# Regrouping the last batch's dense pieces, an earlier gather and a late register read in a fused sparse-attention and expert kernel

## Chip, cores and metric

The kernel runs on one NeuronCore of a Trainium2 chip. The metric is the device time of one execution in microseconds. The median of three runs of the kernel before is 246.15 us (246.1 to 246.69).

## What is computed

A chunk-sparse causal attention, then a layer of eight experts with a dense residual branch. Cut to what matters:

```python
# attention: q, k, v are (4, 8, 768, 64); chunks of 32 keys, the 6 best chunks per query
ub = sum(maximum(q * k_min, q * k_max))           # bound of a chunk's scores
top_chunks = argsort(where(causal, ub, -1e9))[..., -6:]
attn = softmax(where(in_top_chunk & (i >= j), q @ k.T / 8, -1e9))
x = (attn @ v) as rows (3072 tokens, 512)

# experts: 8 experts, 512 -> 512 -> 512, each token goes to one
y_dense = relu(x @ w1_dense) @ w2_dense
e = argmax(x @ w_gate, axis=1); gate_w = softmax(x @ w_gate)[e]
y_moe[mask_e] = gate_w * (relu(x[mask_e] @ w1[e]) @ w2[e])
out = y_dense + y_moe                              # (3072, 512) float32
```

## The kernel before

**Attention.** The four batches run one after the other, each as four pairs of heads. Between the attention steps of a batch the expert layer's work on the batch before is interleaved: transposes of x, the gate, the ranks of the tokens within their experts, and the dense branch. For every token its row of x, its gate weight and its token number are scattered into a table in DRAM, sorted by expert. What is left after the last attention step is the last batch's share of this work and all expert blocks.

**Expert blocks.** The table is read in blocks of 128 rows, each of one expert. `N1 = 11` blocks are full before the last batch is known; up to `N2 = 20` more follow. `NOFT = 28` blocks are always done; three rare ones stand in a conditional at the end, `tc.If(total > N2 - RARE)`, where `total` is a count that the program computes (`nblk`) and that every engine reads into a register. For block i the steps are:

- `fetch(i)` (line 498): SyncE loads the block's rows from the table into `xg`; the last block, 27, has a tile `xl` of its own and is fetched ahead of 11 (`order`).
- `own(i)` (line 513): VectorE copies the expert's first weights to a fixed place (`w`).
- `tx(i)` (line 856): TensorE transposes the rows, VectorE copies them out (858).
- `e1(i)` (865): sixteen matmuls of the first layer; ScalarE applies relu (868).
- `e2(i)` (886): four matmuls of the second layer; ScalarE multiplies by the gate weight (893); GpSimd scatters the 128 result rows and adds them to the output in DRAM (895).

TensorE's program order in loop step i is e1(i), tx(i+1), the step's extra work, e2(i-1).

**The extra work.** The last batch's dense branch is 28 pieces: two groups of 384 tokens, each eight half pieces of the first layer (408, two matmuls each) and six half pieces of the second layer (424, two matmuls each). Every second piece of the second layer ends in a ScalarE copy to a tile `ys` (429) and two SyncE writes to the output (433). The pieces are dealt to loop steps from 1 on by the line with `extra.setdefault`. In steps 0 to 2 also stand the last batch's transposes, gate, ranks, its six table scatters (388) on GpSimd, and SyncE's eight writes of empty rows to the table (914).

**Orders that are written out.** Fetches of blocks from 11 on begin in step 8, and each is ordered behind the latest dense write emitted so far (`latest["ys"]`). SyncE works its queue in order. GpSimd's scatters are in block order.

**The last block's dense rows.** The scatter of block 27 doesn't add: `dense_rows(27)` (878) gathers the dense results of its 128 tokens from the output beforehand into `dr`, on GpSimd's queue behind the latest scatter, and VectorE adds them (891) before the scatter, which overwrites. The gather must find all dense writes of the batch done. It stands in step 12.

**The count.** In step 9 all five engines read `nblk` (line 954; a TENSOR_LOAD in each engine's own queue). A similar read (line 470) fetches the packed list of experts, on TensorE and VectorE, in step 8 for the blocks from 11 on.

Of the kernel before, what the change touches and what calls it, by code (L numbers as in the profile page):

```python
# [7 lines left out]

# [9 lines left out]
def kernel(  # L18
# [12 lines left out]
    nc = tc.nc  # L31
# [25 lines left out]
    N1 = (N * (B - 1) // B - E * 127 + 127) // 128  # L57
    N2 = NBLK - N1
# [107 lines left out]
    nblk = const.tile([1, 1], mybir.dt.int32)  # L166
# [80 lines left out]
    def apart(dma, group, reason):  # L247

        if group in groups:
            tc.declare_no_dep(dma.ins, group=group, reason=reason)  # L250
        groups.add(group)
        tc.add_to_no_dep_group(group, dma.ins)
# [227 lines left out]
    def load_offs():  # L480

        for have, engine in ((offs, mybir.EngineType.PE), (offs1, mybir.EngineType.DVE)):
            have.extend(unpack((eo, eparts[engine]), EF, 3, NK * 512, engine, (E - 1) * NK * 512,
                               "the expert of a block is at most the last"))
# [7 lines left out]
    def fetch(i):  # L492
        if i == NBLK - RARE - 1:
            xg = eg.tile([128, XW], U16, name="xl", bufs=1)
        else:
            xg = eg.tile([128, XW], U16, name="xg")
        es[i]["x"] = xg
        ld = nc.sync.dma_start(out=xg, in_=table[bass.ds(rows[i], 128)])
        if i < N1:
            tc.add_to_no_dep_group("full", ld.ins)  # L500
# [5 lines left out]
    def own(i):  # L506
        if i < 1:
            w = eg.tile([128, NK, 512], HF, name="w1a", bufs=1)
        else:
            w = later[0].tile([128, NK, 512], HF, name="w1", bufs=2)  # L510
        es[i]["w1"] = w
        with tc.issue_after(latest["xT"].ins) if "xT" in latest else nullcontext():
            nc.vector.tensor_copy(w.rearrange("p j f -> p (j f)"), w1f[:, bass.ds(offs1[i], NK * 512)])  # L513

    FIRST = 6
    with (
# [131 lines left out]
        h = None  # L648
        for d16, src in ((k16, s0["k"]), (q16, s0["q"])):
            o = d16.rearrange("p t g d -> p g t d")  # L650
            nc.gpsimd.tensor_copy(o[:, :, 0:3], src[:, :, 0:3])
            with after(h) if h else ExitStack():
                h = nc.scalar.copy(o[:, :, 3:6], src[:, :, 3:6])
            if src is s0["k"]:
                with after(h):
                    h = nc.scalar.copy(kT[0][0][64:128], exf)
# [27 lines left out]
        def place_k(p, g, pk):  # L684
            return nc.scalar.copy(kT[p][g][64 * g : 64 * g + 64].rearrange("d (T p j) -> d T p j", p=128, j=NJ),
                                  pk[64 * g : 64 * g + 64].rearrange("d (T j p) -> d T p j", p=128, j=NJ))
# [9 lines left out]
        with after(h):  # L696
            h = nc.scalar.activation(qp, pq, AF.Relu)
# [4 lines left out]
        for g in range(2):  # L702
            with after(h):
                h = place_k(0, g, pk)
        with after(dv):
            prep_ub(0)
        with after(h):
            h = nc.scalar.copy(kT[0][1][0:64], exf)
# [26 lines left out]
        with after(scored[-1][1]):  # L735
            h = nc.scalar.activation(qp, pq, AF.Relu)
# [102 lines left out]
    with (  # L839
# [8 lines left out]
        a, d, ranks, places, _ = batch_fills(B - 1)  # L848
# [3 lines left out]
        def tx(i):  # L852
            s = es[i]
            tp = p1.tile([128, NK, 128], HF, name="tp", tag="tr")
            for ko in range(NK):
                nc.tensor.transpose(tp[:, ko], s["x"][:, ko * 128 : (ko + 1) * 128].bitcast(HF), ident)  # L856
            s["xT"] = xT = et.tile([128, NK, 128], HF, name="exT")
            latest["xT"] = nc.vector.tensor_copy(xT, tp)  # L858

        def e1(i):  # L860
            s = es[i]
            hp = p2.tile([128, NK, 128], FP, name="hp", tag="h")
            for j in range(NK):
                for ko in range(NK):
                    nc.tensor.matmul(hp[:, j], s["w1"][:, ko, j * 128 : (j + 1) * 128], s["xT"][:, ko],  # L865
                                     start=(ko == 0), stop=(ko == NK - 1), skip_group_check=True)
            s["hT"] = h = et.tile([128, NK, 128], HF, name="ehT")
            nc.scalar.activation(h, hp, AF.Relu)  # L868

        def tokens(i):  # L870
            return bass.IndirectOffsetOnAxis(ap=es[i]["x"][:, Dm + 2 : Dm + 4].bitcast(mybir.dt.int32), axis=0)

        def dense_rows(i):

            es[i]["dense"] = dr = et.tile([128, Dm], FP, name="dr", bufs=1)
            nc.gpsimd.memset(dr, 0.0)
            with tc.issue_after(latest["pool"].ins):
                ga = nc.gpsimd.indirect_dma_start(out=dr, out_offset=None, in_=out, in_offset=tokens(i),
                                                  bounds_check=N - 1, oob_is_err=False)
            apart(ga, "add", "every token is in one block")  # L880

        def e2(i):
            s = es[i]
            yp = p3.tile([128, Dm], FP, name="yp", tag="y")
            for j in range(NK):
                nc.tensor.matmul(yp, s["hT"][:, j], w2f[:, bass.ds(offs[i] + j * 512, 512)],  # L886
                                 start=(j == 0), stop=(j == NK - 1))
            o = et.tile([128, Dm], FP, name="yo", bufs=5)
            gate, to = s["x"][:, Dm : Dm + 2].bitcast(FP), tokens(i)
            if "dense" in s:  # L890
                nc.vector.scalar_tensor_tensor(o, yp, gate, s["dense"], ALU.mult, ALU.add)
            else:
                nc.scalar.mul(o, yp, gate)  # L893
            with tc.issue_after(latest["put"].ins) if i == 0 else nullcontext():
                sc = nc.gpsimd.indirect_dma_start(out=out, out_offset=to, in_=o, in_offset=None, bounds_check=N - 1,  # L895
                                                  oob_is_err=False,
                                                  compute_op=ALU.bypass if "dense" in s else ALU.add)
            latest["pool"] = sc
            apart(sc, "add", "every token is in one block")
            if i < N1:  # L900
                tc.declare_no_dep(sc.ins, group="dense", reason="the first blocks hold no token of the last batch")
                tc.add_to_no_dep_group("add1", sc.ins)

        def empty():
# [7 lines left out]
            for e in range(E):  # L912
# [2 lines left out]
                apart(z, "rows", "these rows are no token's")  # L915
                tc.declare_no_dep(z.ins, group="full", reason="the first blocks end before these rows")

        AHEAD = 8
        READY = 8
        for i in range(1, 1):  # L920
# [2 lines left out]
        extra = {0: a[:NT] + [a[NT], ranks], 1: list(places)}  # L923
        extra[2] = [empty]
        for n, f in enumerate(d):
            extra.setdefault(1 + n * (N1 - 2) // len(d), []).append(f)
        got = FIRST

        NOFT = NBLK - RARE
# [1 line left out]
        for i in range(NOFT):  # L931
            while got < min(i + AHEAD + 2 + (i >= READY), NOFT, N1 + 3 * max(i - READY + 1, 0)):
                if got < N1:
                    fetch(order[got])
                else:
                    with tc.issue_after(latest["ys"].ins):
                        fetch(order[got])
                got += 1
            if 1 <= i + 1 < NOFT:
                own(i + 1)  # L940
            e1(i)
            if i + 1 < NOFT:
                tx(i + 1)
            for f in extra.get(i, ()):
                f()
            if i > 0:
                e2(i - 1)
            if len(offs) < min(i + 4, NBLK):
                load_offs()
            if i == N1 + 1:  # L950
                dense_rows(NOFT - 1)
            if i == READY + 1:
                with tc.issue_after(latest["rows"].ins):
                    total = nc.values_load_multi_w_load_instructions(
                        nblk, min_val=0, max_val=N2, bass_reorder=False,
                        skip_runtime_bounds_check_because="the blocks that are left are at most N2")[1][0]
        e2(NOFT - 1)
        with tc.If(total > N2 - RARE):
            for i in range(NOFT, NBLK):
                fetch(i)  # L960
                latest.pop("xT", None)
                own(i)
                tx(i)
                e1(i)
                e2(i)
# [30 lines left out]
```

## Time and profile before

| | |
|---|---|
| median of 3 runs | 246.15 us |
| profiled execution, its own time | 247.56 us |
| its span, first to last instruction | 245.9 us |
| mean granted TensorE clock | 0.983 |
| TensorE busy | 211.6 us (86%) |
| VectorE busy | 175.4 us (71%) |
| ScalarE busy | 174.3 us (71%) |
| GpSimd busy | 162.9 us (66%) |
| DMA | 50.55 MB, mean 206 GB/s |

The chain of waits follows the work that ended last back to the start, each step to what released it; "issue" in it is time in which an engine waited for nothing that the profile shows. In a timeline, the bracket behind a row is the idle time of that engine before it and what ended it. POOL is GpSimd, PE TensorE, DVE VectorE, ACT ScalarE, SP SyncE; a q behind the name means the engine's instruction queue. L886 is line 886 of the kernel before.

### The profile page before, as it was taken

Reading aid. Unit: us, or ns where it says so; the run is one execution under the profiler, and the core shown is the slowest. Engines: PE = TensorE matmul, PEld = TensorE weight load, DVE = VectorE, ACT = ScalarE, POOL = GpSimd, SP = SyncE. Lnnn points to the kernel's source line nnn. Section 1 sums busy time; section 2 is a strip of 40 time slices with the busy share of each in tenths; the row PEclk is TensorE's granted clock in tenths of the full one; section 3 lists DMA queues with packets and bytes.
Section 4 is the critical chain, followed back from the end, with each engine's and each line's share of the span. In section 5 each row is a group of like instructions: output and inputs, shape, how many; then the busy total and the mean of one; then the engine's idle time right before and its main releaser. Section 6 shows DMA issues by size and latency. Waiting matters only on the chain.

```text
span 245.9 us, 7890 instructions
## 1 busy us (share of the span) xinstructions
PE 211.6 (86%) x2771; PEld 149.6 (61%) x2771; DVE 175.4 (71%) x561; ACT 174.3 (71%) x325; POOL 162.9 (66%) x213
## 2 busy tenths in 40 slices
PE   1688878898997999988999996989999989999950
PEld 0466556676666676755667764667666557777720
DVE  3889999999989789797798996577723335555510
ACT  4579797897887898696899786644556556666630
POOL 6457997785379687268877517330688757888881
PEclk9999999999999999999999998899999999999996
DMA  6999999999899999979999946147589999968785
GB/s 174 247 268 279 210 240 251 270 214 265 222 168 358 182 300 261 263 128 251 296 177 256 188 82 182 42 119 197 157 267 215 222 250 254 204 130 122 88 122 106
DMA packets 68279, 50.55 MB, mean 206 GB/s; under 512 B 29712, under 2 KB 61328, under 8 KB 68240
## 3 DMA queue, kind: packets, MB, share of 16 engines
q1 hardware_dynamic: 53008, 30.72, 47.0%
q0 software_dynamic: 15232, 19.32, 45.8%
q8 instruction: 23, 0.38, 0.6%
q14 instruction: 16, 0.13, 0.2%
HBM read 41.93 MB, written 18.23 MB: 245 GB/s over the span
## 4 chain that ended last, share of the span: by engine, by line
PE 35%; POOL 16%; DVE 14%; issue 12%; ACT 10%; DMA 10%; POOLq 1%; SPq 0%; DVEq 0%; ACTq 0%
ACT ex L608 6%; PE yp L886 6%; PE hp L865 6%; PE hp L408 5%; POOL ex L610 4%; DMA out_dram<-yo,xg 4%; DVE ks L546 4%; PE sp L604 4%; POOL table L388 4%; PE yp L424 4%; DMA xg<-table 2%; PE op L623 2%; DMA qf<-in_q_dram 2%; ACT kp L543 2%; PE tp L856 2%
## 5 line engine op out<-in xcount | busy, mean ns | idle before, releaser
L608 ACT ACTIVATE ex<-sp 128x512 f16<-128x512 f32 (+1 forms) x176 | 91.5, 613 | 10.3 <-PE sp L604 8.5
L604 PE MATMUL sp<-rT,kT 128*128 128x128 f16 (+3 forms) x384 | 64.3, 262 | 4.3 <-ACT ex L608 1.1
L610 POOL TENSOR_SCALAR_AFFINE_SELECT ex<-ex 128x512 f16<-128x512 f16 x48 | 32.4, 685 | 37.7 <-ACT ex L608 25.6
L895 POOL DMA_INDIRECT out_dram<-yo,xg x27 | 44.8, 1660 | 12.0 <-issue 5.2
L623 PE MATMUL op<-v,ex 128*128 128x65 f16 x672 | 45.9, 194 | 7.2 <-POOL ex L610 5.6
L623 PEld LDWEIGHTS <-ex 128*128 128x128 f16 x672 | 35.9, 98 | 23.1 <-POOL ex L610 10.0
L388 POOL DMA_INDIRECT table<-xbig,slot x24 | 24.3, 1012 | 18.5 <-issue 18.5
L858 DVE COPY exT<-tp 128x512 f16<-128x512 f16 x28 | 11.8, 423 | 32.8 <-PE tp L856 31.5
L604 PEld LDWEIGHTS <-kT 128*128 128x128 f16 x384 | 28.5, 98 | 8.4 <-issue 5.2
L886 PE MATMUL yp<-we,ehT 128*128 x112 | 30.9, 379 | 0.4 <-ACT ys L429 0.2
L865 PEld LDWEIGHTS <-w 128*128 128x128 f16 x432 | 26.4, 98 | 7.9 <-issue 2.2
L408 PE MATMUL hp<-xT,wd 128*128 128x384 f16 x128 | 30.2, 341 | 0.6 <-DVE xT L264 0.6
L865 PE MATMUL hp<-exT,w 128*128 128x128 f16 x432 | 29.2, 219 | 0.7 <-issue 0.7
L893 ACT ACTIVATE yo<-yp,xg 128x512 f32<-128x512 f32 x27 | 18.5, 687 | 14.0 <-PE yp L886 13.2
L546 DVE TENSOR_REDUCE ks<-kp 128x24 f16<-128x768 f16 x28 | 25.5, 945 | 3.7 <-ACT kp L543 3.5
L424 PE MATMUL yp<-wd,hT 128*128 128x512 f16 x96 | 25.7, 379 | 0.3
L868 ACT ACTIVATE ehT<-hp 128x512 f16<-128x512 f32 x28 | 16.7, 597 | 12.1 <-PE hp L865 9.0
L413 ACT ACTIVATE hT<-hp 128x384 f16<-128x384 f32 x30 | 15.0, 498 | 12.0 <-PE hp L408 11.4
L513 DVE COPY w<-we 128x2048 f16 x27 | 18.7, 693 | 0.2 <-DVE exT L858 0.2
L634 DVE TENSOR_TENSOR xbig<-op,rs 128x384 f16<-128x384 f32 x32 | 17.5, 547 | 0.3
L429 ACT COPY ys<-yp 128x512 f32<-128x512 f32 x21 | 12.8, 609 | 6.3 <-PE yp L424 6.0
L886 PEld LDWEIGHTS <-ehT 128*128 128x128 f16 x112 | 10.2, 97 | 10.3 <-issue 3.6
(158 smaller groups left out, 371.6 us busy)
## 6 DMA issues: line engine op xcount, KB each, us to landing
we<-in_moe_w_dram POOLq DMA_DIRECT2D x16, 512.0 KB, 6.6
kf<-in_k_dram SPq DMA_DIRECT2D x32, 192.0 KB
qf<-in_q_dram SPq DMA_DIRECT2D x32, 192.0 KB
vf<-in_v_dram SPq DMA_DIRECT2D x32, 192.0 KB
out_dram<-ys SPq DMA_DIRECT2D x48, 128.0 KB
xg<-table SPq DMA_DIRECT2D x27, 136.0 KB
table<-zt SPq DMA_DIRECT2D x9, 136.0 KB
wd<-in_moe_w_dense_dram POOLq DMA_DIRECT2D x2, 512.0 KB, 6.3
```

What stands on the lines that cost most here:

```text
L388: sc = nc.gpsimd.indirect_dma_start(out=table, out_offset=bass.IndirectOffsetOnAxis(ap=keep["slot"][:, t : t + 1], axis=0), in_=xbig[b % 2 ...
L408: nc.tensor.matmul(hp, wd[:, ko, j * 128 : (j + 1) * 128], xT[:, ko, g * G * 128 : (g + 1) * G * 128], start=(ko == 0), stop=(ko == NK - 1))
L424: nc.tensor.matmul(yp, hold["h"][:, j, i * 128 : (i + 1) * 128], wd[:, NK + j], start=(j == 0), stop=(j == NK - 1))
L513: nc.vector.tensor_copy(w.rearrange("p j f -> p (j f)"), w1f[:, bass.ds(offs1[i], NK * 512)])
L546: nc.vector.tensor_reduce(out=ks[:, i], in_=kp.rearrange("d (c w) -> d c w", w=32), op=op, axis=mybir.AxisListType.X)
L604: last = nc.tensor.matmul(sp[:, o : o + w], kT[p % NB][g][:, kt * 128 : (kt + 1) * 128], rT[p % NB][g][:, a * 128 : z * 128], start=(o == ...
L608: scored.append((last, nc.scalar.activation(ex[:, 0:o], sp[:, 0:o], AF.Exp, scale=-0.125)))
L610: latest["pool"] = nc.gpsimd.affine_select(out=ex, in_=ex, compare_op=ALU.is_ge, fill=0.0, base=0, pattern=[[0, 4], [1, 2], [2, 64]], chan ...
L623: nc.tensor.matmul(s["op", g][:, t * (D + 1) : (t + 1) * (D + 1)], ex[:, o : o + 128], v16[p % NB][:, g, kt, :], start=first, stop=(last_o ...
L865: nc.tensor.matmul(hp[:, j], s["w1"][:, ko, j * 128 : (j + 1) * 128], s["xT"][:, ko], start=(ko == 0), stop=(ko == NK - 1), skip_group_che ...
L886: nc.tensor.matmul(yp, s["hT"][:, j], w2f[:, bass.ds(offs[i] + j * 512, 512)], start=(j == 0), stop=(j == NK - 1))
L895: sc = nc.gpsimd.indirect_dma_start(out=out, out_offset=to, in_=o, in_offset=None, bounds_check=N - 1, oob_is_err=False, compute_op=ALU.by ...
```

## The change

Three edits. The 28 dense pieces of the last batch are dealt to seven loop steps (1 to 7) instead of nine (1 to 9), four to each. The gather of the last block's dense rows moves from step 12, behind the scatter of block 11, to step 10, behind the scatter of block 9, the tenth. TensorE's read of the block count moves from step 9 to behind the last e2; the other engines keep theirs in step 9, and the registers of both reads are put together into one value for the conditional.

```diff
+        def count(engines):
+            return nc.values_load_multi_w_load_instructions(
+                nblk, engines=engines, min_val=0, max_val=N2, bass_reorder=False,
+                skip_runtime_bounds_check_because="the blocks that are left are at most N2")[1][0]
+
+        def both(a, z):
+            hs = [h for v in (a, z) for h in (v.val.handles if hasattr(v.val, "handles") else (v.val,))]
+            return RuntimeValue.of_register_unchecked(RegisterHandles(tuple(hs)), min_val=0, max_val=N2)
...
         for n, f in enumerate(d):
-            extra.setdefault(1 + n * (N1 - 2) // len(d), []).append(f)
+            extra.setdefault(1 + n * (N1 - 4) // len(d), []).append(f)
...
-            if i == N1 + 1:
+            if i == N1 - 1:
                 dense_rows(NOFT - 1)
             if i == READY + 1:
                 with tc.issue_after(latest["rows"].ins):
-                    total = nc.values_load_multi_w_load_instructions(
-                        nblk, min_val=0, max_val=N2, bass_reorder=False,
-                        skip_runtime_bounds_check_because="the blocks that are left are at most N2")[1][0]
+                    total = count([e for e in mybir.ALL_ENGINES if e != mybir.EngineType.PE])
         e2(NOFT - 1)
+        total = both(total, count([mybir.EngineType.PE]))
         with tc.If(total > N2 - RARE):
```

More of the change, by code (lines that the diff above doesn't have):

```diff
@@ L5 @@
 from concourse import bass_utils, mybir
+from concourse.bass_primitives_rust import RegisterHandles
+from concourse.expressions import RuntimeValue
 from concourse.masks import make_identity, make_upper_triangular
```

## The prediction, made before the changed kernel was run

> **What bounds the kernel now.** I read the page first, then the chain of waits from 160 us on, then each queue's timeline over the expert stage (165 us to the end), and last the time that transfers took to land. The change touches only that stage. TensorE sets its pace. The first line is from the page, the rest are rows of the chain (start, length, both us), where e1 is line 865, tx 856, e2 886, dense pieces 408 and 424:
>
> ```profile
> PE 211.6 (86%) x2771; PEld 149.6 (61%) x2771; DVE 175.4 (71%) x561; ACT 174.3 (71%) x325; POOL 162.9 (66%) x213
> ...
> 192.31 0.89 PE hp L865 x16
> ...
> 193.43 0.88 PE yp L424 x4
> ...
> 194.33 0.59 ACT ys L429
> ...
> 195.99 0.89 PE hp L865 x16
> ...
> 197.11 1.29 PE yp L424 x6
> 198.40 1.17 PE yp L886 x4
> 199.57 0.68 issue
> 200.25 1.05 PE hp L865 x16
> ...
> 206.35 0.89 PE hp L865 x16
> ...
> 207.47 0.86 PE yp L886 x4
> 208.33 0.89 PE hp L865 x16
> ```
>
> A block without dense pieces takes 1.98 us (206.35 to 208.33). Blocks 8 and 9 carry three second-layer pieces each, six matmuls, 1.29 us. The 0.68 us at 199.57 is the one place where TensorE stands still in this stretch with its data there. The answer for the count's tile names the reason, and the one for line 470 shows a second read of the same kind:
>
> ```profile
> L954 PEldq TENSOR_LOAD <-nblk x1: 992/992/992, 199.2 to 199.2; - x1
> L470 PEldq TENSOR_LOAD <-eo x2: 830/982/1134, 149.3 to 193.1; - x2
> ```
>
> A register read of 0.99 us at 199.2 runs past the queued e2 matmuls, which end at 199.57. The read of the expert list at 193.1 does the same for up to 1.13 us, but behind four second-layer matmuls (193.43, 0.88 us), and costs nothing that the chain shows.
>
> At the very end GpSimd is the last engine, not TensorE:
>
> ```profile
> 205.55 1.57 POOL L895 DMA_INDIRECT out_dram<-yo,xg  x1 [0.61 <-ACT yo L893]
> 207.43 1.56 POOL L895 DMA_INDIRECT out_dram<-yo,xg  x1 [0.30 <-DMA xg<-table]
> 209.29 1.33 POOL L878 DMA_INDIRECT dr<-out_dram,xl  x1 [0.30 <-issue]
> 210.93 1.68 POOL L895 DMA_INDIRECT out_dram<-yo,xg  x1 [0.30 <-issue]
> 212.91 1.64 POOL L895 DMA_INDIRECT out_dram<-yo,xg  x1 [0.30 <-issue]
> 213.78 0.69 DVE L513 COPY w<-we 128x2048 f16 x1
> 214.86 1.67 POOL L895 DMA_INDIRECT out_dram<-yo,xg  x1 [0.30 <-issue]
> ...
> 234.11 0.69 ACT L893 ACTIVATE yo<-yp,xg 128x512 f32<-128x512 f32 x1 [0.43 <-PE yp L886]
> 235.86 0.69 ACT L893 ACTIVATE yo<-yp,xg 128x512 f32<-128x512 f32 x1 [0.21 <-PE yp L886]
> 236.00 1.36 PE L886 MATMUL yp<-we,ehT 128*128 x4 [0.17 <-issue]
> 237.46 0.75 DVE L891 SCALAR_TENSOR_TENSOR yo<-yp,xl,dr 128x512 f32<-128x512 f32 x1 [3.79 <-PEq L958]
> 238.25 1.55 POOL L895 DMA_INDIRECT out_dram<-yo,xg  x1 [0.31 <-issue]
> 240.11 1.03 POOL L895 DMA_INDIRECT out_dram<-yo,xl  x1 [0.30 <-issue]
> ```
>
> The gather at 209.29 costs GpSimd 1.64 us (0.30 + 1.33) and puts it a block behind. It stays behind: its free step is 1.56 + 0.30 = 1.86 us, but with the lag it ends 0.08 us after VectorE's weight copy ends (212.91 + 1.64 = 214.55 against 213.78 + 0.69 = 214.47) and steps with it, 1.95 to 1.98 us. So the last scatter starts at 240.11, 1.90 us after its operand is ready (237.46 + 0.75 = 238.21).
>
> **The change part by part.** *The count on TensorE last.* The four other engines keep their reads. Without the one at 199.2 block 10 starts 0.68 us earlier: **-0.68**. At the end the same read, 0.99 us, follows e2 of the last block (ends 237.36). Even if the last VectorE instruction had to wait for what stands behind it (its releaser is written as TensorE's queue at line 958), its result would come at 238.21 + 0.99 = 239.20, still before the scatter's slot at 240.11. Cost 0, covered by GpSimd's lag; without that lag up to 0.99 us would show.
>
> *Dense pieces over seven blocks.* Twenty-eight pieces go four each to blocks 1 to 7, instead of 4 and eight times 3 to blocks 1 to 9. No matmul is added. Block 9 took 199.57 - 195.99 = 3.58 us from its first chain row, of which 1.98 are the block and 1.29 the pieces, so 0.31 us is friction (e2 takes 1.17 instead of 0.86); block 8 took 3.68, friction 0.41 with the wait for line 429. Two blocks lose such friction, six that gain a piece may have more: I take **-0.35**, ends -0.72 and 0. But block 8 loses the cover of the expert-list read. By the count's read, 0.68 shown of 0.99, it would cost 0.68 x 1.134 / 0.992 = 0.78; where it is placed earlier, 0. I take **+0.5**.
>
> So block 8 starts at 199.57 - 0.35 - 2 x 1.98 = 195.26 (before 192.31), block 10 at 195.26 + 0.5 + 3.96 = 199.72, and tx(11), which comes 0.89 us into it, is due at 200.61. Before, it ran at 201.14. Up to here the sum is **-0.53**.
>
> *What the regrouping does to SyncE's queue.* This is the step that decides. In block 8 the loop fetches the last block's rows (xl), then 11 and 12, each ordered behind the latest dense write so far. Before, that was the last write of the first half:
>
> ```profile
> 182.62 4.23 SPq L433 DMA_DIRECT2D out_dram<-ys  x6
> 187.29 0.99 SPq L498 DMA_DIRECT2D xl<-table  x1
> 188.55 1.39 SPq L498 DMA_DIRECT2D xg<-table  x2
> 194.94 1.12 SPq L433 DMA_DIRECT2D out_dram<-ys  x2
> 196.48 2.17 SPq L498 DMA_DIRECT2D xg<-table  x3
> 198.44 0.59 ACT L429 COPY ys<-yp 128x512 f32<-128x512 f32 x1 [0.28 <-DMA out_dram<-ys]
> 201.14 0.39 PE L856 MATMUL tp<-ident,xg 128*128 128x128 f16 x4
> ```
>
> Block 11's rows were asked for at 188.55 and used at 201.14: 12.6 us of room. Now all 28 pieces are emitted before block 8, so the fetches stand behind the last of the twelve dense writes. Its tile is ready 199.57 - (198.44 + 0.59) = 0.54 us before the block after next starts, so now at 195.26 - 0.54 = 194.72. Two writes and the step to the next fetch take 196.48 - 194.94 = 1.54 us, xl 0.72 (2.17 / 3) to 1.26 (188.55 - 187.29): block 11 is asked for at 197.0 to 197.5; I take 197.2. How long does it take to land?
>
> ```profile
> 162.35 2.34 DMA xg<-table
> 212.82 3.72 DMA xg<-table
> 195.00:200.00 5.00, 4.57 (x34) 2.35 (x33) 1.02 (x2) 2.85 (x5) 2.47 (x2) 1.00 1.12 228
> 210.00:215.00 5.00, 5.00 (x67) 3.94 (x65) 2.59 (x5) 3.25 (x5) 4.08 (x4) 1.00 0.91 195
> DMA to landing us min/median/max: 6.5/7.0/7.4
> DMA to landing us min/median/max: 4.3/4.7/5.5
> ```
>
> Two fetches in the chain; then busy time by stretch, where the last two columns are the share of the 16 DMA engines and GB/s; then the landing times of the scatters of line 895 in 185 to 204 us and in 209 to 232 us. Alone a fetch takes 2.34 us, at a DMA share of 0.91 3.72, and the dense stretch is at 1.12. There scatters land 7.0 / 4.7 = 1.5 times later, which would make a fetch 5.5. The new stretch holds six dense writes close together, but its scatters come no faster than TensorE's blocks: I take 4.6, the middle of 3.72 and 5.5; ends 2.34 and 7.0. It lands at 197.2 + 4.6 = 201.8, so tx(11) waits 1.2 us and runs 201.8 - 201.14 = **0.66 us later than before**. A later start of block 8 moves this step by as much. Behind tx(11) on TensorE stand e2(9) and e1(11), and all later blocks. Block 12's rows come about 0.7 us after block 11's and are due 1.98 us after; the rest have more room, so the wait happens once.
>
> The Trainium skill ("DMA: Bandwidth & Descriptors", Anatomy of one DMA) fits a transfer issued by GpSimd as 2.0 us plus bytes over 436e3 per us. By an estimate from it 136 KB would land in 2.3 us, near the lone fetch, and tx(11) would not wait at all: the sum would be -0.53, 245.6. The lone fetch of 2.34 agrees with it, the one of 3.72 under load does not.
>
> *The gather behind the tenth scatter.* It needs the twelve dense writes landed; the last is issued near 195.4 and even with 7.0 us lands near 202.4. Scatter 9 has its operand from e2(9), after tx(11), so about 204, and the gather issues behind it: no wait, or a few tenths. Its 1.64 us again stand between two scatters whose operands come 1.98 us apart, with the same phase to the weight copies: lag again a block, two blocks sooner, and held by the same lock. Worth 0; ends -1.29 (no lag left: the operand of the last scatter but two is ready at 234.11 + 0.69 = 234.80, its scatter at 235.10, and the last 2 x 1.86 later at 238.82 instead of 240.11) and +0.3. xl itself lands by about 201 and is first read by the gather.
>
> Sum: -0.68 - 0.35 + 0.5 + 1.19 (the wait) + 0 = **+0.66**, say +0.7. The profiled execution took 247.56 (span 245.9), 1.4 above the median of 246.15; on it the sum is 248.3, on the median **246.85**.
>
> **The rivals.** *In time* (0.22): the fetch takes up to 3.4 us. Then -0.53, or -1.03 if the expert-list read is hidden too: 245.1 to 245.6. For it: the lone 2.34. Against it: the share of 1.12. It decides below 200.61 - 197.2 = 3.4 us. The fit of the Trainium skill's page "DMA: Bandwidth & Descriptors" leads here.
>
> *The lag goes* (0.18): the other side. If TensorE's order has e2(9) ahead of tx(11), as its order already mixes matmuls of neighbouring steps elsewhere, scatter 9 and the gather run while TensorE waits, 0.86 us of the wait is used, and GpSimd is no longer behind: 0.66 - 0.86 - 1.29 = -1.5, so 244.7. It decides if the wait exceeds e2's 0.86 us. Against it: in every late block of the trace e2 follows tx.
>
> *Landing like a scatter* (0.10): 7.0 us, 204.2, so +3.1: 249.2. For it: both go through the same full DMA engines.
>
> **How the numbers follow.** No change can be told within 0.3%, 0.74 us. The forecast itself has 0.50, with its own range 245.9 to 247.7 (fetch 3.7 to 5.5 us): 0.27 of it slower by more than 0.74, 0.23 within. In time: 0.13 faster, 0.09 within. The lag goes: 0.18 faster. Landing like a scatter: 0.10 slower. Together 0.31 faster, 0.32 same, 0.37 slower. The range 244.9 to 248.2 leaves out most of the slowest case and the lower half of the lag case.
>
> **What the new profile would show.** Right: no idle of TensorE from a count read near 199; a read of 1 us in TensorE's queue at the end, with GpSimd's last scatter still waiting for nothing; blocks 8 and 9 near 2 us; SyncE's xl and block 11 fetches behind the last dense write, near 196 to 198; TensorE idle before line 856 at about 200.6, released by a transfer from the table; GpSimd's steps after the gather still 1.95 to 1.98. Wrong: no idle at line 856 (in time), GpSimd's steps with idle behind ScalarE up to the end (the lag goes), an idle of over 2 us, or fetches that stand ahead of the dense writes after all.

## The result, and the profile after

The changed kernel takes 248.95 us (median of 6 runs, 248.56 to 250.24) against 246.44 us (median of 6, 246.10 to 248.03) of the kernel before beside it: ratio 1.0101, 95% interval 1.0069 to 1.0132, so 1.7 to 3.3 us slower. Here and below the ratios compare the fast executions alone, so they need not be the quotient of the two medians beside them. The forecast was 246.85 us, +0.7, with a range up to 248.2. The result lies above the range.

"Before" and "after" stand for the two kernels below. The line numbers of after used here are those of before plus two: e1 is line 867, tx 858, e2 888, the dense pieces 410 and 426, the dense writes 435, the scatter 897, the gather 880, the fetch 500. First the page:

```profile
span 247.0 us, 7890 instructions
...
PE 210.5 (85%) x2771; PEld 150.4 (61%) x2771; DVE 175.1 (71%) x561; ACT 174.6 (71%) x325; POOL 161.8 (66%) x213
```

TensorE does the same instructions and is busy 1.1 us less in a span 1.1 us longer: what was added is waiting. The chain of waits shows where (start, length, both us):

```profile
189.65 1.73 PE yp L426 x8
191.37 1.15 PE yp L888 x4
...
192.54 0.70 ACT yo L895
...
193.24 0.33 SPq L435
...
193.62 0.95 SPq L435
...
194.99 0.36 SPq L500
...
195.64 5.13 DMA xg<-table
```

The chain leaves TensorE after the last dense pieces (189.65) and the e2 behind them, runs through ScalarE's multiply of that block (192.54) and SyncE's last two dense writes (435), then the fetch of the last block's rows (194.99), and then 5.13 us through the fetch of block 11, up to its transposes at 200.81. Before, no fetch of a table block stood on the chain between 185 and 212 us. TensorE's timeline in the same stretch (the bracket is the idle time before the row, and what ended it):

```profile
192.34 1.05 PE L867 MATMUL hp<-exT,w 128*128 128x128 f16 x16
...
195.28 1.05 PE L867 MATMUL hp<-exT,w 128*128 128x128 f16 x16 [0.79 <-DVE w L515]
...
197.25 1.06 PE L867 MATMUL hp<-exT,w 128*128 128x128 f16 x16
200.81 0.49 PE L858 MATMUL tp<-ident,xg 128*128 128x128 f16 x4 [2.50 <-DMA xg<-table]
201.18 1.87 PE L888 MATMUL yp<-we,ehT 128*128 x4
202.84 1.80 PE L867 MATMUL hp<-exT,w 128*128 128x128 f16 x16
204.48 0.39 PE L858 MATMUL tp<-ident,xg 128*128 128x128 f16 x4
```

TensorE stands still for 2.50 us ahead of the transposes of block 11, and the next steps take 1.87 and 1.80 us for what is 1.03 and 1.06 elsewhere. The windows around it say why (the columns: length, busy time of PE, its weight loads, DVE, ACT, POOL with instruction counts, granted clock, DMA share, GB/s):

```profile
197.00:199.00 2.00, 1.31 (x18) 0.98 (x16) 0.61 (x2) 1.30 (x3) 0.62 (x2) 1.00 0.89 190
199.00:201.00 2.00, 0.19 (x4) 0.19 (x5) 0.00 (x0) 0.00 (x1) 0.97 (x1) 0.99 1.10 264
201.00:203.00 2.00, 2.00 (x10) 0.87 (x8) 1.02 (x2) 0.00 (x0) 0.00 (x0) 0.50 1.11 293
203.00:205.00 2.00, 2.00 (x23) 1.88 (x21) 0.10 (x1) 0.95 (x2) 0.95 (x1) 0.65 1.04 306
```

Right behind the idle the granted clock is 0.50. The loss in the last three rows is 2 x (0.01 + 0.50 + 0.35) = 1.72 us of full clock, so the clock was halved for about 3.4 us. From tx(11) to tx(12) TensorE takes 204.48 - 200.81 = 3.67 us instead of 1.98.

GpSimd's timeline around the gather and at the end, VectorE's last row, and the answers for the count's tile and for the list of experts:

```profile
204.05 1.97 POOL L897 DMA_INDIRECT out_dram<-yo,xg  x1 [4.08 <-ACT yo L895]
206.32 1.08 POOL L880 DMA_INDIRECT dr<-out_dram,xl  x1 [0.30 <-DMA xg<-table]
...
240.94 1.03 POOL L897 DMA_INDIRECT out_dram<-yo,xl  x1 [0.30 <-issue]
```
```profile
238.82 0.75 DVE L893 SCALAR_TENSOR_TENSOR yo<-yp,xl,dr 128x512 f32<-128x512 f32 x1 [3.79 <-PE yp L888]
```
```profile
L921 PEldq TENSOR_LOAD <-nblk x1: 1004/1004/1004, 238.3 to 238.3; - x1
L472 PEldq TENSOR_LOAD <-eo x2: 810/1336/1861, 149.1 to 193.4; - x2
```

The gather waits for no more than the 0.30 us that GpSimd's other steps show too. The last scatter starts 240.94 - (238.82 + 0.75) = 1.37 us after its operand is ready; before it was 1.90. TensorE's read of the count now starts at 238.3, and VectorE's last addition begins before it ends. The read of the list is 1.86 us long at its second place: it ends at 193.4 + 1.86 = 195.26, and e1(9) starts at 195.28, so TensorE was held by the read. The bracket of that row names VectorE's weight copy.

The two profiled executions must be laid over each other at the second transposes of the expert stage, tx(1), since before's had lost time earlier. It took 247.56, 1.1 above the median of 246.44, and shows a halved clock at the end of attention, where no line of this change works. The rows are before's window, then tx(1) before and after:

```profile
153.00:156.00 3.00, 3.00 (x17) 1.52 (x16) 1.95 (x5) 0.98 (x2) 0.07 (x1) 0.54 0.16 52
```
```profile
164.73 0.40 PE L856 MATMUL tp<-ident,xg 128*128 128x128 f16 x4 [0.67 <-DMA xg<-table]
```
```profile
163.22 0.40 PE L858 MATMUL tp<-ident,xg 128*128 128x128 f16 x4 [0.86 <-DMA xg<-table]
```

From tx(1) to the end of the last scatter's row, before takes 240.11 + 1.03 - 164.73 = 76.41 us and after 240.94 + 1.03 - 163.22 = 78.75: +2.34, which agrees with the medians' +2.5. To compare a time after with one before, 1.51 us (164.73 - 163.22) is added to it below.

### The profile page after: what moved, and what is told of

It reads as the page before. It is cut to its first block, busy times and chain, and to the rows that moved or that the text cites. A ratio compares the mean times of both kernels' runs of the same rounds, so it can differ in the third digit from the quotient of the medians.

```text
span 247.0 us, 7890 instructions
## 1 busy us (share of the span) xinstructions
PE 210.5 (85%) x2771; PEld 150.4 (61%) x2771; DVE 175.1 (71%) x561; ACT 174.6 (71%) x325; POOL 161.8 (66%) x213
## 4 chain that ended last, share of the span: by engine, by line
PE 34%; POOL 17%; DVE 14%; DMA 13%; ACT 9%; issue 8%; SPq 1%; POOLq 1%; ACTq 0%
PE hp L867 8%; PE yp L888 7%; ACT ex L610 6%; DMA out_dram<-yo,xg 5%; POOL table L390 4%; DVE ks L548 4%; POOL ex L612 4%; PE hp L410 4%; DMA xg<-table 3%; PE sp L606 3%; PE yp L426 2%; DMA we<-in_moe_w_dram 2%; DMA qf<-in_q_dram 2%; PE tp L858 2%; ACT kp L545 2%
## 5 line engine op out<-in xcount | busy, mean ns | idle before, releaser
L867 PEld LDWEIGHTS <-w 128*128 128x128 f16 x432 | 27.2, 100 | 7.8 <-DVE w L515 1.5
L867 PE MATMUL hp<-exT,w 128*128 128x128 f16 x432 | 29.8, 222 | 0.8 <-DVE w L515 0.8
L410 PE MATMUL hp<-xT,wd 128*128 128x384 f16 x128 | 28.3, 326 | 0.6 <-DVE xT L266 0.6
```

The source lines that it names most:

```text
L410: nc.tensor.matmul(hp, wd[:, ko, j * 128 : (j + 1) * 128], xT[:, ko, g * G * 128 : (g + 1) * G * 128], start=(ko == 0), stop=(ko == NK - 1))
```

## Experiments

Theory A: the fetches that the regrouping put behind the last dense write make TensorE wait for block 11's rows, and that is the loss. Rivals: the loss is in another of the three edits (B), or in the halved clock behind the idle rather than in the idle (C).

**Each edit alone.** The count on TensorE last, in the kernel before:

```
-                    total = nc.values_load_multi_w_load_instructions(... all engines ...)
+                    total = count([e for e in mybir.ALL_ENGINES if e != mybir.EngineType.PE])
         e2(NOFT - 1)
+        total = both(total, count([mybir.EngineType.PE]))
```

> The kernel before with one of the three edits: TensorE reads the block count behind the last e2. Theory (the fetch of block 11 behind the last dense write, and the half clock after TensorE's idle, cost the time): this part alone is a gain, block 10 starts about 0.7 us earlier, the last GpSimd scatter too, so -0.7 us against before (-0.3 to -1.0). Rival (the late read, or the early gather, holds up the end): 0 or slower.

246.06 us against 246.88: ratio 0.9968 (0.9940 to 0.9995), -0.8 us (-1.5 to -0.1), as the forecast's -0.68.

The dense pieces over seven blocks, in the kernel before (`N1 - 2` to `N1 - 4`, nothing else):

> The kernel before with one edit: dense pieces dealt to steps 1 to 7. Gather in step 12 and TensorE's count read in step 9 as before. Theory: the fetch of block 11 again stands behind the twelfth dense write, lands about 5 us later and tx(11) waits; TensorE's count read lies inside that wait and costs nothing more. About +2.5 us if the clock halves after the idle as in the changed kernel, +1.0 if the shorter idle (about 1.8 us) leaves the clock alone. Rival (the gather is what costs): 0 or a gain, with no idle before tx(11).

250.36 us: ratio 1.0118 (1.0074 to 1.0163), +2.9 us (1.8 to 4.0). TensorE's timeline has the same stop at block 11, and windows the same clock (0.50 in the window shown; this execution had a further halving elsewhere, so only this place is read):

```profile
206.26 0.61 PE L856 MATMUL tp<-ident,xg 128*128 128x128 f16 x4 [2.53 <-DMA xg<-table]
```
```profile
207.00:209.00 2.00, 2.00 (x10) 1.08 (x9) 0.93 (x2) 0.39 (x1) 0.00 (x0) 0.50 1.09 254
```

The gather in step 10, in the kernel before (`N1 + 1` to `N1 - 1`, nothing else):

> The kernel before with one edit: the gather in step 10, behind the tenth scatter; pieces over nine steps, TensorE's count read in step 9. Theory (the gather costs GpSimd one block wherever it stands): it waits for the last dense write to land (about 206 after the start in the profile of before) and then holds up scatter 10; TensorE is not touched; lag of a block or a little more as before; 0 to +0.5 us against before. Rival (the early gather is what costs in the changed kernel): +1 us or more.

247.81 us against 246.64: ratio 1.0039 (1.0011 to 1.0066), +1.0 us (0.3 to 1.6). The forecast had 0 with +0.3 as the upper end; the interval begins there. GpSimd's last row and tx(1):

```profile
240.68 1.03 POOL L895 DMA_INDIRECT out_dram<-yo,xl  x1 [0.30 <-issue]
```
```profile
165.00 0.40 PE L856 MATMUL tp<-ident,xg 128*128 128x128 f16 x4 [0.57 <-DMA xg<-table]
```

The sum of the three edits alone is -0.8 + 2.9 + 1.0 = +3.1, and together they measured +2.5. B is out as the main cause: the dense edit alone loses all of it. The early gather alone lost more than was expected of it; that stays open.

**The fetches earlier, all else as after.** The fetches of the last block and of 11 and 12 go to step 6, ahead of the last six of the twelve dense writes:

```
-            while got < min(..., N1 + 3 * max(i - READY + 1, 0)):
+            while got < min(..., N1 + 3 * max(i - READY + 1, int(i >= 6))):
```

> The changed kernel with the fetches of the last block, 11 and 12 taken from step 8 to step 6, so that they stand ahead of the second half's dense writes in SyncE's queue; nothing else moves. Theory: no idle before tx(11), no half clock near 201 us after the start; tx(11) runs when due, 1.5 us earlier than in the kernel before, so about -4 us against the changed kernel and -1.5 us (-0.8 to -2.2) against before. Rival (early gather or late read): the loss of 2.5 us stays, or most of it.

245.62 us against 246.88: ratio 0.9958 (0.9929 to 0.9988), -1.0 us (-1.8 to -0.3); 3.5 us better than after's ratio, with one number in one line. TensorE's timeline, and the window behind the idle in it:

```profile
195.97 1.05 PE L867 MATMUL hp<-exT,w 128*128 128x128 f16 x16 [1.11 <-DVE w L515]
...
198.84 0.39 PE L858 MATMUL tp<-ident,xg 128*128 128x128 f16 x4
```
```profile
197.00:199.00 2.00, 2.00 (x28) 1.53 (x26) 1.02 (x2) 1.28 (x2) 0.41 (x1) 1.00 1.08 260
```

TensorE runs block 11's transposes (198.84) without a wait, and the clock is 1.00. A is shown: where the fetches stand is the loss. The gain is smaller than the -1.5 expected. An idle of 1.11 us remains at 195.97, behind the read of the list of experts; how much of the shortfall it is was not shown here.

**The clock held up while TensorE waits.** After, with eleven matmuls of 128x512 whose result nobody uses between e1(10) and tx(11):

```
+            if i == N1 - 1:
+                spin(11)
```

> The changed kernel with eleven extra 128x512 matmuls on TensorE (about 2.4 us, their result is never read) between e1(10) and tx(11), where it waits for block 11. Theory (the idle itself makes the clock fall to half for 3.4 us, worth 1.5 us): tx(11) runs at the same time as in the changed kernel, the clock stays at 1.0, e2(9) and e1(11) take 0.9 us each; -1.5 us against the changed kernel, +1.0 against before. Rival (the clock falls for another reason, or its fall is hidden by GpSimd's lag): same time as the changed kernel.

249.31 us against 246.88: ratio 1.0087 (1.0055 to 1.0118), +2.2 us. The expected 1.5 us were not gained. The timeline (in this version e2 is line 895 and the scatter 904), with tx(1) ahead of it:

```profile
165.18 0.40 PE L858 MATMUL tp<-ident,xg 128*128 128x128 f16 x4 [0.58 <-DMA xg<-table]
...
200.84 2.54 PE L877 MATMUL spin<-wd 128*128 128x512 f16 x11
203.68 0.40 PE L858 MATMUL tp<-ident,xg 128*128 128x128 f16 x4 [0.30 <-DMA xg<-table]
...
206.10 0.39 PE L858 MATMUL tp<-ident,xg 128*128 128x128 f16 x4
```

The slow spell is gone: tx(11) to tx(12) takes 206.10 - 203.68 = 2.42 us instead of 3.67. But two things take the gain back. The fetch took longer in this execution's chain of waits, and GpSimd's last scatter starts 243.08 - (240.49 + 0.75) = 1.84 us behind its operand, where after has 1.37. The chain's row, then GpSimd's and VectorE's last:

```profile
197.98 5.66 DMA xg<-table
```
```profile
243.08 1.03 POOL L904 DMA_INDIRECT out_dram<-yo,xl  x1 [0.30 <-issue]
```
```profile
240.49 0.75 DVE L900 SCALAR_TENSOR_TENSOR yo<-yp,xl,dr 128x512 f32<-128x512 f32 x1 [3.84 <-PE yp L895]
```

This execution is the slowest of its nine, 250.92 us, but from tx(1) to the end of the last scatter's row it takes 243.08 + 1.03 - 165.18 = 78.93 us, with no spell of half clock, and after takes 78.75 with one. Block 11 was asked for later here (197.98 - 165.18 = 32.80 us behind tx(1), in after 32.42) and landed later, so tx(11) itself ran 2.09 us later than before, measured from tx(1) (38.50 against 36.41).

The other executions of after point the same way. A spell of 3.4 us at half takes 0.007 off the mean granted clock (1.7 of 247.0 us). The profiled executions of all versions without a spell ahead of their end have a mean of 0.987 to 0.992, those with one or more 0.969 to 0.984. One of after's six has 0.989, so no spell, and took 248.91 us.

So the halved clock, C, is not the main cause. Its net share lies between nothing and about 1.4 us (0.35 us between the two ratios, and 1.1 for their intervals of 0.8 each), and stays open within that.

**One issue earlier.** After, with block 11 fetched ahead of the last block (`order = [*range(N1 + 1), NOFT - 1, *range(N1 + 1, NOFT - 1)]`):

> After, with block 11's rows fetched ahead of the last block's instead of behind them: block 11 is asked for one SyncE issue (0.65 us) earlier and nothing else moves. If the wait at the transposes of block 11 decides and each us of it is paid once, tx(11) runs about 0.65 us earlier, TensorE's idle there is about 1.85 us instead of 2.50, and the kernel is 0.4 to 0.9 us faster than after, +1.6 to +2.1 against before. If the half clock hangs on the length of this idle and is paid in full, the shorter idle leaves the clock at 1.0 and the gain is 0.65 + 1.5 = 2.1 us, +0.4 against before. If the landing is set by the load on the DMA engines and not by the time of issue, the fetch lands at the same time as in after, and nothing is gained.

249.17 us against 246.73: ratio 1.0077 (1.0045 to 1.0109), +1.9 us, 0.6 below after's ratio, in the direction and size of the first theory, but the intervals overlap, so it is not shown. The idle is 1.98 us, and the clock falls again:

```profile
202.21 0.40 PE L858 MATMUL tp<-ident,xg 128*128 128x128 f16 x4 [1.98 <-DMA xg<-table]
```
```profile
203.00:205.00 2.00, 2.00 (x13) 1.26 (x13) 0.67 (x2) 0.69 (x1) 0.00 (x0) 0.58 1.13 283
```

**The list of experts read earlier.** First in the version with the early fetches, with one read more in step 7:

```
             for f in extra.get(i, ()):
                 f()
+            if i == 7:
+                load_offs()
             if i > 0:
                 e2(i - 1)
```

> The kernel with the early fetches (step 6), and TensorE's and VectorE's read of the expert list placed in step 7 between the dense pieces and e2(6), so that eight second-layer matmuls are queued on TensorE ahead of it. Theory (without dense pieces behind it the read stops TensorE for about 1 us in block 8): no idle of TensorE before e1(9), -1.0 us (-0.6 to -1.2) against the early fetches alone, about -2 us against before. Rival (that idle is VectorE's weight copy, as the profile writes it): same as the early fetches alone.

245.17 us against 246.64: ratio 0.9940 (0.9912 to 0.9968), -1.5 us (-2.2 to -0.8). The expected -1.0 against the version without it came out as about -0.4, which the two intervals don't tell from nothing. The timeline shows where it may have gone: the idle ahead of e1(9), which the profile had put down to VectorE's copy, is gone with the read, but at its new place the read, 2.3 us in the answer for its line, leaves 0.73 us of idle there (the bracket names ScalarE's copy), behind eight dense matmuls:

```profile
L472 PEldq TENSOR_LOAD <-eo x2: 805/1554/2303, 149.5 to 189.7; - x2
```
```profile
189.84 1.89 PE L426 MATMUL yp<-wd,hT 128*128 128x512 f16 x8
192.47 1.36 PE L888 MATMUL yp<-we,ehT 128*128 x4 [0.73 <-ACT ys L431]
```

Then the same edit with the fetches left late, as in after:

> After, with the read of the list of experts of block 9's step brought forward to step 7, ahead of e2(6), as in the version that also fetched early, but with the fetches left where after has them. There the earlier read was worth 0.45 us. If block 11's rows set the end, TensorE only waits longer for them: its idle ahead of tx(11) grows by what the read no longer costs (from 2.5 to between 2.9 and 3.5 us), tx(11) runs at the same time behind the last dense write, and the time is that of after within 0.5 us, about +2.5 against before. If the loss is a sum of independent stalls, the kernel is 0.45 to 1.0 us faster than after.

250.03 us against 246.73: ratio 1.0142 (1.0090 to 1.0194), +2.2 to +4.8. Not faster than after, as the theory has it, by which TensorE only waits away what it saves ahead of block 11's rows. That longer wait is not shown: the profiled execution is the fastest of its six, 247.15 us (the next took 248.59). Rows of SyncE's and TensorE's timelines and the windows around them:

```profile
196.62 3.24 SPq L500 DMA_DIRECT2D xg<-table  x5
```
```profile
199.54 0.40 PE L858 MATMUL tp<-ident,xg 128*128 128x128 f16 x4
```
```profile
197.00:199.00 2.00, 2.00 (x29) 1.53 (x26) 1.02 (x2) 1.30 (x3) 1.58 (x2) 1.00 0.97 216
199.00:201.00 2.00, 2.00 (x20) 1.14 (x18) 1.02 (x2) 1.08 (x2) 1.57 (x2) 1.00 1.11 259
```

Here the fetch was there within 199.54 - 196.62 = 2.9 us, TensorE did not wait and the clock stayed at 1.00. The same kind of fetch from the same place in the queue took 5.13 and 5.66 us in the executions above. The landing time varies between executions, and what sets it stays open.

**Is the gather worth its place, or worth anything?** The version with early fetches and early list, first with the gather back in step 12, then without it, so that the last scatter adds like the others:

> As the run with early fetches and the moved list read, but the gather back in step 12. Theory (GpSimd's lag is one block either way, held by the weight copies): same time within 0.3 us. Rival (the earlier gather lets GpSimd catch up, or holds it up): 0.5 us or more apart.

> As the run with early fetches and the moved list read, without the gather: the last block's rows are added by its scatter like the others'. Theory (the lag comes from the gather's step alone): GpSimd's scatters start about 0.3 us after their operands up to the last blocks, the last but two about 1.3 us earlier; the last scatter takes 1.55 instead of 1.03 us and lands later as an adding one does; together -0.3 us (-1.0 to +0.3) against the run with it. Rival (the lag has another cause): the scatters stay 1.8 us behind.

245.22 us, ratio 0.9947 (0.9923 to 0.9971), and 245.31 us, ratio 0.9942 (0.9917 to 0.9968): both as the version with the gather in step 10 (0.9940). GpSimd's last rows, with the gather in step 10 and without it:

```profile
237.48 1.03 POOL L897 DMA_INDIRECT out_dram<-yo,xl  x1 [0.30 <-issue]
```
```profile
236.11 1.55 POOL L897 DMA_INDIRECT out_dram<-yo,xl  x1 [0.30 <-issue]
```

Without the gather GpSimd isn't a block behind, and the last scatter starts 1.4 us sooner in spans of the same length (242.9 and 243.0 us). From its start to the end it takes 243.0 - 236.1 = 6.9 us when it adds, and 242.9 - 237.5 = 5.4 us when it overwrites. The gather buys 1.5 us of landing and pays for it with its lag.

## Why the prediction was wrong

**The count (-0.68; measured -0.8 alone) and the late read (0)** were right. The idle of 0.68 us is gone. At the end the read runs from 238.3 to 239.3, and the last scatter, at 240.94, comes behind GpSimd's own queue.

**Friction of the dense pieces (-0.35) was too small.** Block 10 started at 197.25, in before's time 198.76, so 1.49 us before the 200.25 of before; the forecast had 0.53. With the count's -0.68 and the list's +0.95 (next point) the friction gave -1.49 + 0.68 - 0.95 = -1.76. Half of it came from the two freed blocks, half from the early ones that took a fourth piece. Before's rows for e1(8) and e1(10):

```profile
192.15 1.06 PE L865 MATMUL hp<-exT,w 128*128 128x128 f16 x16
...
200.25 1.05 PE L865 MATMUL hp<-exT,w 128*128 128x128 f16 x16 [0.68 <-issue]
```

Between them lie 8.10 us: 3.96 for two blocks, 2.58 for six pieces, 0.68 for the read, and 0.88 of friction, where the forecast counted 0.31 + 0.41. From tx(1) to e1(8) before takes 27.42 us and after 29.12, so 1.70 more for six pieces more of 2.58 us: another 0.88 less friction, where the forecast had expected more. The windows of 22 us from tx(1) on, before and then after:

```profile
165.00:187.00 22.00, 21.98 (x249) 14.99 (x247) 12.97 (x48) 11.39 (x21) 11.10 (x9) 1.00 0.73 202
```
```profile
163.50:185.50 22.00, 22.00 (x257) 15.71 (x254) 12.64 (x47) 12.31 (x23) 11.07 (x9) 1.00 0.74 205
```

TensorE counts as busy all the time in both, yet it does eight matmuls, four pieces, more in the second: "busy" hid the slack.

**The list of experts (+0.5)** lost its cover as forecast, and cost more: block 9's start shows 0.79 us of idle, and from e1(8) to e1(10) (192.34 to 197.25 in the timeline) it takes 4.91 us instead of 2 x 1.98, so 0.95. The read itself was 1.86 us long (the largest of its two), not the 1.13 of before.

**SyncE's queue** came out at the forecast's time, in part by luck. The fetch of block 11 was asked for at 195.64, in before's time 197.15; the forecast had 197.2. But the last dense tile was ready earlier than forecast, and its write stood longer:

```profile
191.41 0.58 ACT L431 COPY ys<-yp 128x512 f32<-128x512 f32 x1 [0.28 <-PE yp L426]
```

The copy ends at 191.99, in before's time 193.50, where the forecast had 194.72. Its two writes are asked for from 193.24 on, when ScalarE's multiply of block 7 ends, which the chain names as what released them. Why they should wait for it stays open.

**The landing (4.6 us) and the wait (1.2 us) were too small.** It took 5.13 us, so tx(11) ran at 200.81 + 1.51 = 202.32 instead of the 201.8 forecast: 1.18 us later than before, not 0.66. That is 0.5 us of the miss. The fetch of 2.34 us that the forecast calls lone was not alone: from 162.30 to 164.70 the DMA share was 0.57. The rest of the idle, 2.50 instead of 1.2, is TensorE's earlier readiness (198.31, in before's time 199.82, instead of 200.61), which costs nothing by itself. What comes next stands right behind this idle.

**The step that failed: the price of block 11's wait, 0.66 us, with "the wait happens once".** I let all later blocks follow at 1.98 us. In the profiled execution the clock halved behind the idle, and tx(11) to tx(12) took 3.67 us, 1.69 more. GpSimd gave 0.53 of it back (1.90 - 1.37). So 1.18 + 1.69 - 0.53 = 2.34, the whole difference of the stage. The Trainium skill ("TensorE: Matmul & The Clock Gate", Part 1) says that the clock falls to half after an idle window of about 3.4 us, and warns of gaps longer than that. Here the trace agrees on the half (0.50), and the slow spell is as long (about 3.4 us), but idles of 2.50 and 1.98 us stood ahead of it, and one of 1.11 us was followed by none; the measurement decides.

The halving is not needed for the loss, though. In the version with matmuls in the gap it is gone and the stage is as long, because tx(11) itself ran 2.09 us later and tx(11) to tx(12) took 0.44 more (2.42). What both executions share is that rows asked for behind the last dense write cost over 2 us, by a later landing (5.13 and 5.66 us instead of 4.6) and by what follows it. How much of the medians' +2.5 us is the landing and how much the clock stays open.

**The gather (0)**: in the changed kernel it behaved as drawn, without a wait of its own beyond the queue's step, in the room that the slow clock left. Alone it cost 0.3 to 1.6 us; in its profile the stage from tx(1) (165.00) to the end of the last scatter's row (240.68 + 1.03) takes 76.71 us, 0.3 more than before. What more there may be is open. With the fetches early, steps 10 and 12 took the same time (245.17 and 245.22 us).

**The rivals.** *Landing like a scatter* came nearest in its time, 249.2, for a reason of its own: in the profiled execution not a landing of 7.0 us but 5.13 and the clock. *In time* happened in one execution, with the list read early, at 2.9 us of landing. *The lag goes* did not: in after, e2(9) stands behind tx(11), and GpSimd keeps a lag.

## What to carry to other kernels

When work is regrouped, look for everything that is ordered by "the latest so far": here the dense writes' order held the fetches, and one line's number (fetch from step 6 instead of 8) turned +2.5 us into -1.0. A wait in front of TensorE can have a spell of half clock behind it, which a forecast must allow for beside its length, though what the spell costs net was not settled here. And less work ahead of a wait for a transfer gained nothing here until the transfer was asked for earlier. The best version found here, with the early fetches and the early list, takes 245.17 us, 1.5 us (0.8 to 2.2) below the kernel before.

## What was not expected of the hardware

- An idle of TensorE of 1.98 us was followed by a granted clock of 0.58 in a window of 2 us, one of 2.50 by about 3.4 us at half.
- The same fetch of 128 table rows landed within 2.9 us in one execution, with DMA shares of 0.97 and 1.11 around it, and in 5.13 in another, with shares of 0.89 (197 to 199 us) and 1.10 (199 to 201). The share of busy DMA engines did not tell here how long a transfer takes; I had read the landing from it.
- A register read in TensorE's queue took 0.8 to 2.5 us for the same instruction. The profile gives the idle behind it to VectorE's copy (after), to ScalarE's (the list read early) or to "issue" (before).
